# Caps, norms and residual adds of a fused attention block moved from VectorE to GpSimd

## The chip, the core and the metric

The kernel runs on one core of a Trainium2 chip. A core has TensorE (PE, the matrix engine, which writes to PSUM), VectorE (DVE) and GpSimd (POOL) for elementwise work, ScalarE (ACT) for activation functions, and SyncE (SP), whose queue issues most of the DMAs here. Each engine takes its own instructions in order; between engines they wait on semaphores. The metric is the device time of one execution in microseconds (us): the median of several runs.

## The reference

`x` is [1, 2048, 640] in bf16. Rows are normalised, and two branches work on the result: linear attention with 32 heads of 20 channels, and a dense network with a ReLU, 1728 wide, whose output goes through a SiLU and gates the attention.

```python
def _layernorm(x, axis=-1, eps=1e-5):
    m = jnp.mean(x, axis=axis, keepdims=True)
    v = jnp.var(x, axis=axis, keepdims=True)
    return (x - m) / jnp.sqrt(v + eps)
...
        phi = lambda t: jnp.where(t > 0, t + 1, jnp.exp(t)) + 1e-6
        pq, pk = phi(q), phi(k)
        kv = jnp.einsum("bhsd,bhse->bhde", pk, v)
        z = jnp.einsum("bhsd->bhd", pk)
        num = jnp.einsum("bhqd,bhde->bhqe", pq, kv)
        den = jnp.einsum("bhqd,bhd->bhq", pq, z)[..., None] + 1e-6
        o = num / den
...
    xn = _layernorm(x, axis=-1)
    s = _A_ref(xn, A_wqkv, A_wo)
    g = _silu(_B_ref(xn, B_w1, B_w2))
    return x + s * g
```

The kernel computes `phi(t)` as min(exp(t), 1) + 1e-6 + relu(t): ScalarE takes the exponential and the ReLU out of PSUM, one instruction makes the cap (the minimum and the small addend), and one adds the two parts.

## The kernel before

**Tiles.** The 2048 rows are 16 tiles `t` of 128 rows, and four chunks `j` of 512. Each tile of `x` is loaded, `bn_stats` (L469) and `bn_aggr` (L473) on VectorE give its mean and variance, GpSimd makes the reciprocal root with two small instructions (`rsv` L475, `rsy` L477), and `LN_norm` (L497) writes the normalised tile `xn`. A DMA from the SP queue (L546) transposes it to `xnT`. The first four tiles are centred early and transposed on TensorE instead.

**Keys.** `K_mm` (L556) multiplies a tile by the key weights into two PSUM banks. `K_exp` and `K_relu` (L569, ScalarE) write to one of three or four slots of `ek`, and `K_fin(t)` makes the cap in place (L585) and the sum into `pk` (L587). All of `pk` is read much later, by the sum over the keys (L756) and by the products of `xn` and `pk` (L882, from 105 us).

**Queries.** `Q_mm` (L609) does the same for a chunk and 128 channels: ScalarE writes the exponential to one of three slots `er` (L617) and the ReLU to `pqT` (L622), then `f_sum` makes the cap (L630) and the sum (L827, the line of the helper `tt` for every elementwise operation with two tensors).

**Strassen units.** The products are made with Strassen's method in a form of seven products: sums of input blocks (`h_S`, `h_T`, `g_S`, `u_S`, `o_S`, all recorded at L827) are formed on VectorE, and products are gathered in PSUM. The hidden layer has ten such units (`h_unit`, matmuls at L1036): four for the first half of the rows (33 to 60 us), six for the second (70 to 112 us). A unit has the steps `s1`, `s5`, `s6`, `s2`, `s7`, `s3`, `s4`. In `s6`, VectorE adds a saved product to a PSUM bank that the next products of `s7` and `s3` write again; in `s4` it makes another such sum and a ReLU. Between the steps the key products of a tile, a query product and pieces of other work are put in by hand, as lists: in the first four units `first` holds the norms of tiles 10 to 15 (with `post`), `misc` and `post` the statistics of tiles 11 to 15, and `rest` and `fill_` go on with this up to 96 us.

**The last stage.** From 128 us on, pairs of tiles go through the second layer (`U_steps`), ScalarE's SiLU gate (L1354) and the output product (`O_steps`), both in PSUM banks by the same seven steps (L882). `s_mult` (L1517) multiplies the output product in PSUM by the gate into one of three slots `tmpo`; `s_store` (L1522) adds the rows of `x`, which were loaded again to `xre`, into a slot `outb`, and a DMA from the SP queue stores them. The adds of a pair are put off to the first step of the next pair (`late`, `flush`). The last tile goes in three pieces, the first of which GpSimd adds and ScalarE's queue stores.

**Order and waits.** The class `Sched` records each operation on the engine named in the call, in the order of the calls, and derives the semaphore waits from the reads and writes that the call names. So the order on an engine is the order of the program, and moving an operation to another engine changes neither the order of the calls nor what each of them depends on.

Of the kernel before, what the change touches and what calls it, by code (L numbers as in the profile page):

```python
# [4 lines left out]
ALU = mybir.AluOpType  # L5
# [203 lines left out]
def bass_recurrent_scan__linear_attn_block__dense_activation_relu__prompt_kernel(  # L209
# [78 lines left out]
    def eks(t):  # L288
        return t % 4 if t < 8 else t % 3
# [63 lines left out]
    sc = Sched(nc, NDS)  # L353
    nds = [0]

    def dma(E, fn, R=(), W=(), extra=()):
        i = nds[0]
        nds[0] += 1
        return sc.dma(E, fn, i, R=R, W=W, extra=extra)

    def tok(t):
        return slice(P * t, P * (t + 1))

    def schunk(j):
        return slice(512 * j, 512 * (j + 1))
# [3 lines left out]
    def xs(t):  # L369
        return t if t < XR else (t - 4) % XR  # L370
# [114 lines left out]
    last_norm = [None]  # L485

    def LN_norm(t):
        if t >= 99:
            sc.op("POOL", lambda eng: eng.scalar_tensor_tensor(
                out=rsv[:, t:t + 1], in0=mv[:, t, 0:1], scalar=-1.0, in1=rsy[:, t:t + 1], op0=ALU.mult, op1=ALU.mult),  # L490
                R=[("mv", t), ("rsy", t)], W=[("rsv", t)])
            last_norm[0] = sc.op("ACT", lambda eng: eng.activation(
                out=xn[:, t, :], in_=xin[:, xs(t), :], func=ACTF.Identity, bias=rsv[:, t:t + 1],
                scale=rsy[:, t:t + 1]), R=[("xin", xs(t)), ("rsv", t), ("rsy", t)], W=[("xn", t)])
            xnT_dma(t)
            return
        last_norm[0] = sc.op("DVE", lambda eng: eng.tensor_scalar(  # L497
            out=xn[:, t, :], in0=xin[:, xs(t), :], scalar1=mv[:, t, 0:1], scalar2=rsy[:, t:t + 1],
            op0=ALU.subtract, op1=ALU.mult), R=[("xin", xs(t)), ("mv", t), ("rsy", t)], W=[("xn", t)])
        xnT_dma(t)  # L500
# [44 lines left out]
    def xnT_dma(t):  # L545
        dma("SP", lambda eng: eng.dma_start_transpose(  # L546
            xnT[:, t // 4, :, P * (t % 4):P * (t % 4 + 1)], xn[:, t, :]), R=[("xn", t)], W=[("xnT", t)])
# [33 lines left out]
    def K_fin(t):  # L581
        es = eks(t)
        e_ = ek[:, es, 0, :]
        r_ = ek[:, es, 1, :]
        sc.op("DVE", lambda eng: eng.tensor_scalar(out=e_, in0=e_, scalar1=1.0, scalar2=1e-6, op0=ALU.min, op1=ALU.add),  # L585
              R=[("ek_e", es)], W=[("ek_e", es)])
        sc.op("DVE", lambda eng: eng.tensor_tensor(out=pk[:, t, :], in0=e_, in1=r_, op=ALU.add),  # L587
              R=[("ek_e", es), ("ek_r", es)], W=[("pk", t)])
# [4 lines left out]
    def nextb():  # L593
        b = RB[ring[0] % len(RB)]
        ring[0] += 1
        return b
# [10 lines left out]
    def Q_mm(j, f, b=None):  # L607
        b = nextb() if b is None else b
        sc.group("PE", [(lambda eng, k=k: eng.matmul(ps[b], lhsT=wq[:, k, P * f:P * (f + 1)], rhs=xnT[:, j, k, :],  # L609
                                                     start=(k == 0), stop=(k == C - 1))) for k in range(C)],  # L610
                 R=[("wq",)] + [("xnT", 4 * j + q) for q in range(4)], W=[("ps", b)])
        es = qi[0] % NER
        qi[0] += 1
        e_ = er[:, es, :]

        def f_exp():
            sc.op("ACT", lambda eng: eng.activation(out=e_, in_=ps[b], func=ACTF.Exp), R=[("ps", b)], W=[("er_e", es)])  # L617

        plain = True

        def f_relu():
            sc.op("ACT", lambda eng: eng.activation(out=pqT[:, f, schunk(j)], in_=ps[b], func=ACTF.Relu), R=[("ps", b)],  # L622
                  W=[("pqT", j, f)], extra=hz(hSk[0:2]) if f == C - 1 and j > 1 else ())

        def f_both():
            f_exp()
            f_relu()

        def f_sum():
            sc.op("DVE", lambda eng: eng.tensor_scalar(out=e_, in0=e_, scalar1=1.0, scalar2=1e-6, op0=ALU.min,  # L630
                                                       op1=ALU.add), R=[("er_e", es)], W=[("er_e", es)])
            tt(pqT[:, f, schunk(j)], e_, pqT[:, f, schunk(j)], ALU.add, [("er_e", es), ("pqT", j, f)], [("pqT", j, f)])

        if plain:
            return f_both, f_sum

        def f_fin():
            sc.op("DVE", lambda eng: eng.tensor_scalar(out=e_, in0=e_, scalar1=1.0, scalar2=1e-6, op0=ALU.min,
                                                       op1=ALU.add), R=[("er_e", es)], W=[("er_e", es)])
            sc.op("DVE", lambda eng: eng.scalar_tensor_tensor(  # L640
                out=pqT[:, f, schunk(j)], in0=ps[b], scalar=1.0 + 1e-6, in1=e_, op0=ALU.add, op1=ALU.max),
                R=[("ps", b), ("er_e", es)], W=[("pqT", j, f)],
                extra=hz(hSk[0:2]) if f == C - 1 and j > 1 else ())

        return f_exp, f_fin
# [101 lines left out]
    def hz(keys):  # L747
        return sc._hazards([], keys)
# [77 lines left out]
    def tt(out, in0, in1, op, R, W, extra=()):  # L826
        sc.op("DVE", lambda eng: eng.tensor_tensor(out=out, in0=in0, in1=in1, op=op), R=R, W=W, extra=extra)  # L827
# [268 lines left out]
    def run(ops):  # L1096
        for op_ in ops:
            op_[0](*op_[1:])

    S, N, F, SH, ZS, T0 = LN_stats, LN_norm, K_fin, h_S, scale_h, h_T  # L1100
    after = [[(S, 5), (N, 4)], [(S, 6), (N, 5)], [(S, 7), (N, 6)], [(F, 0), (N, 7)], [(F, 1)]]
    for n, f in enumerate(HP):
# [44 lines left out]
    for i, u in enumerate(units):  # L1147
        ob = 4 * (i % 2)
        t = 8 + i
# [327 lines left out]
    def O_steps(p):  # L1477
        t0, t1 = pairs[p]
        key = lambda q: ("oS", p % 2, q)
        base = ubase(p)  # L1480

        def prod(i):
            q_ = lambda half, t: [pqT[:, 2 * half + k, tok(t)] for k in range(2)]
            w_ = lambda half, n: [wf[:, 2 * half + k, HN * n:HN * (n + 1)] for k in range(2)]
            s_ = lambda q: [o_Sv(p, q)[:, k, :] for k in range(2)]
            t_ = lambda q: [oT[q][:, k, :] for k in range(2)]
            last = lambda t, n: [(pqT[:, 4, tok(t)], wf[:, 4, HN * n:HN * (n + 1)])]
            z = lambda a, b: list(zip(a, b))
            return {
                1: lambda: (z(q_(0, t0), w_(0, 0)), qk(t0, 0, 2) + wkeys),  # L1490
                2: lambda: (z(q_(1, t0), w_(1, 0)) + last(t0, 0), qk(t0, 2, 5) + wkeys),
                3: lambda: (z(s_(4), w_(1, 1)) + last(t0, 1), [key(4)] + qk(t0, 4, 5) + wkeys),
                4: lambda: (z(q_(1, t1), t_(4)) + last(t1, 0), qk(t1, 2, 5) + wkeys + [("oT", 4)]),
                5: lambda: (z(s_(1), t_(1)), [key(1), ("oT", 1)]),
                6: lambda: (z(s_(2), t_(2)), [key(2), ("oT", 2)]),
                7: lambda: (z(s_(3), t_(3)), [("oS3", p), ("oT", 3)]),
                8: lambda: (last(t1, 1), qk(t1, 4, 5) + wkeys),
            }[i]()

        def out_(q, b, s5=None, skey=None):  # L1500
            if q == 12:
                s_out(t0, base + 2)
            elif q == 21:
                s_out(t1, base)
            elif q == 22:
                tt(ps[b][:, 0:HN], ps[b][:, 0:HN], s5, ALU.add, [("ps", b), skey], [("ps", b)])

        return seven(base, prod, out_, 2 + p % 2, lo8, prod(8))
# [9 lines left out]
            out=tmpo[:, os_, lo:hi].rearrange(shp, a=na), in0=src, in1=g_of(t)[0][:, lo:hi].rearrange(shp, a=na),  # L1518
            op=ALU.mult), R=keys + [("g", gslot[t], 0), ("g", gslot[t], 1)], W=[("tmpo", os_, i)])

    def s_store(t, os_, pieces, lo, hi, E="DVE", D_="SP"):
        sc.op(E, lambda eng: eng.tensor_tensor(out=outb[:, os_, lo:hi], in0=tmpo[:, os_, lo:hi],  # L1522
                                               in1=xre[:, t, lo:hi], op=ALU.add),
              R=[("tmpo", os_, i) for i in pieces] + [("xre", t // 4)], W=[("outb", os_, lo)])
        dma(D_, lambda eng: eng.dma_start(out2[tok(t), lo:hi], outb[:, os_, lo:hi]), R=[("outb", os_, lo)])
# [13 lines left out]
    def s_out(t, b):  # L1539
        os_ = so[0] % NOUT  # L1540
        so[0] += 1
        s_mult(t, os_, 0, 0, D, ps2(b, HN), [("ps", b), ("ps", b + 1)], 2)
        late.append(lambda: s_store(t, os_, (0, ), 0, D))
# [7 lines left out]
    def s_last(t):  # L1551
        for i in range(3):
            lo, hi = LC[i], LC[i + 1]
            s_mm(t, lo, hi, LB[i])
            s_mult(t, NOUT, i, lo, hi, ps[LB[i]][:, 0:hi - lo].unsqueeze(1), [("ps", LB[i])], 1)
            if i == 0:
                s_store(t, NOUT, (0, ), lo, hi, "POOL", "ACT")
        s_store(t, NOUT, (1, 2), LC[1], D)
# [45 lines left out]
    for p in range(8):  # L1604
        us = U_steps(p)
        os_ = O_steps(p - 1) if p else None
# [90 lines left out]
```

## Time and profile before

| what | us |
|---|---|
| median of 3 runs (208.2 to 208.42) | 208.39 |
| span of the profiled execution, from its first to its last instruction | 207.0 |
| TensorE busy | 203.6 |
| VectorE busy | 169.7 |
| ScalarE busy | 124.3 |
| GpSimd busy | 18.0 |

The profile doesn't give the profiled execution a time of its own beside the span; the span is 1.4 us shorter than the median of the runs. By stretches of the span, busy us of each engine:

```profile
core 0: us, PE busy (x) PEld busy (x) DVE busy (x) ACT busy (x) POOL busy (x), PEclk, DMA share, GB/s
24.00:35.50 11.50, 11.50 (x76) 5.37 (x74) 10.09 (x26) 9.01 (x17) 3.27 (x6) 1.00 1.02 253
35.50:41.90 6.40, 6.40 (x35) 3.31 (x34) 5.51 (x15) 5.42 (x11) 0.95 (x2) 1.00 0.41 53
41.90:48.30 6.40, 6.40 (x35) 3.31 (x34) 5.89 (x15) 5.42 (x11) 0.00 (x0) 1.00 0.13 26
48.30:54.70 6.40, 6.40 (x35) 3.31 (x34) 5.50 (x15) 5.42 (x11) 1.58 (x4) 1.00 0.14 28
54.70:60.70 6.00, 6.00 (x33) 3.08 (x32) 4.78 (x13) 4.49 (x9) 2.50 (x10) 1.00 0.27 55
60.70:72.70 12.00, 12.00 (x68) 6.49 (x67) 9.42 (x26) 11.84 (x23) 0.00 (x0) 1.00 0.36 96
72.70:105.00 32.30, 32.30 (x216) 14.78 (x215) 24.93 (x52) 23.35 (x45) 0.00 (x0) 1.00 0.16 49
105.00:146.00 41.00, 41.00 (x314) 28.95 (x312) 35.64 (x55) 17.51 (x37) 0.00 (x0) 1.00 0.67 207
146.00:204.50 58.50, 58.50 (x436) 42.21 (x434) 47.88 (x102) 24.02 (x63) 0.32 (x1) 1.00 0.21 72
```

A row names a stretch from A to B, its length, the busy time and the number of instructions of each engine in it (PEld is TensorE's loading of weights), the clock granted to TensorE, the mean share in which the DMA engines were busy, and what they moved. In the other views a line of a timeline is start, duration, engine, source line, operation, output and inputs with shapes, and in brackets the idle time of the engine before it with what ended it.

### The profile page before, as it was taken

To read this page: it belongs to the slowest core of one execution; us is meant where nothing else is said; L and a number is where in the kernel's file an instruction comes from. 1 tells how busy PE (TensorE), PEld (TensorE's weight loads), DVE (VectorE), ACT (ScalarE), POOL (GpSimd) and SP (SyncE) were. 2 spreads that over 40 slices of the span, in tenths; PEclk is the share of its full clock that TensorE was granted. 3 is DMA by queue.
4 is the path that set the end of the run, shared out by engine and by line. 5 is a ranking of instruction groups with operands and counts; after the bars stand their busy time and mean duration, and the time that the engine had idled before them with its cause. 6 is when DMAs were issued, how large, how long until landed. Compare 5 with 4: busy or idle time off the path is not lost.

```text
span 207.0 us, 3745 instructions
## 1 busy us (share of the span) xinstructions
PE 203.6 (98%) x1400; PEld 126.3 (61%) x1400; DVE 169.7 (82%) x373; ACT 124.3 (60%) x251; POOL 18.0 (9%) x53
## 2 busy tenths in 40 slices
PE   8999999999999999999999999999999999999995
PEld 7755645545555444444456777777777777777773
DVE  4888997988969787686889669898888989897465
ACT  5598869888889987686563435462525354352531
POOL 3174032101330000000000000000000000000001
PEclk9999999999999999999999999999999999999999
DMA  6965999211037000302225999237931011010103
GB/s 194 331 190 117 255 203 275 42 32 29 6 63 198 25 3 0 127 0 57 74 63 114 251 357 384 90 108 234 371 129 63 3 63 46 21 63 0 63 5 127
DMA packets 32999, 24.74 MB, mean 119 GB/s; under 512 B 12757, under 2 KB 32981, under 8 KB 32981
## 3 DMA queue, kind: packets, MB, share of 16 engines
q1 hardware_dynamic: 31749, 23.13, 39.2%
q10 hardware_dynamic: 1232, 1.37, 1.9%
q8 instruction: 11, 0.18, 0.4%
q14 instruction: 7, 0.06, 0.1%
HBM read 15.81 MB, written 5.24 MB: 102 GB/s over the span
## 4 chain that ended last, share of the span: by engine, by line
PE 97%; DMA 1%; DVE 1%; issue 0%
PE psT L882 40%; PE psT L1036 19%; PE psT L556 11%; PE psT L609 11%; PE psT L658 6%; PE psT L1529 3%; PE psT L1580 2%; DMA reg<-in_A_x_dram 1%; PE psT L676 1%; PE psT L1320 1%; PE psT L530 1%; PE psT L1294 1%; PE psT L756 1%; PE psT L786 1%; PE psT L432 0%; DVE stats L469 0%
## 5 line engine op out<-in xcount | busy, mean ns | idle before, releaser
L882 PE MATMUL psT<-reg,regH 128*128 128x320 bf16 (+1 forms) x224 | 34.3, 299 | 0.0
L882 PE MATMUL psT<-reg 128*128 128x320 bf16 (+1 forms) x164 | 27.7, 299 | 0.0
L882 PEld LDWEIGHTS psT<-reg,regH 128*128 128x128 bf16 (+1 forms) x224 | 21.9, 98 | 8.6
L1354 ACT ACTIVATE wv_sb<-psT 128x320 bf16<-128x320 f32 x28 | 11.3, 436 | 25.2 <-PE psT L882 15.4
L609 PE MATMUL psT<-reg 128*128 128x512 bf16 x100 | 24.4, 379 | 0.0
L1036 PE MATMUL psT<-reg 128*128 128x512 bf16 x80 | 23.2, 379 | 0.0
L827 DVE TENSOR_TENSOR psT<-psT,reg 128x320 f32<-128x320 f32 x30 | 14.3, 493 | 9.3 <-PE psT L882 9.2
L889 ACT ACTIVATE psT<-psT 128x320 f32<-128x320 f32 x32 | 13.6, 426 | 11.2 <-PE psT L882 10.7
L882 PEld LDWEIGHTS psT<-reg 128*128 128x128 f16 (+1 forms) x164 | 16.0, 98 | 6.9 <-DVE regH L827 0.2
L889 ACT ACTIVATE reg<-psT 128x320 f32<-128x320 f32 (+1 forms) x24 | 10.4, 435 | 15.6 <-PE psT L882 13.6
L556 PE MATMUL psT<-reg 128*128 128x320 bf16 x120 | 17.9, 299 | 0.0
L1042 ACT ACTIVATE psT<-psT 128x512 f32<-128x512 f32 x20 | 11.9, 595 | 8.2 <-PE psT L1036 8.2
L569 ACT ACTIVATE regE<-psT 128x640 bf16<-128x640 f32 x24 | 15.6, 706 | 1.9 <-PE psT L556 1.2
L609 PEld LDWEIGHTS psT<-reg 128*128 128x128 bf16 x100 | 9.6, 98 | 11.6 <-issue 0.7
L1048 ACT ACTIVATE regH<-psT 128x512 bf16<-128x512 f32 (+1 forms) x24 | 14.5, 604 | 2.1 <-PE psT L1036 1.8
L556 PEld LDWEIGHTS psT<-reg 128*128 128x128 bf16 x120 | 11.5, 98 | 6.5 <-ACT regE L569 0.5
L469 DVE BATCH_NORM_STATS2 stats<-reg 128x6 f32<-128x320 bf16 x32 | 14.1, 475 | 1.3 <-DMA reg<-in_A_x_dram 1.3
L827 DVE TENSOR_TENSOR reg<-reg 128x1024 f16<-128x1024 bf16 (+6 forms) x17 | 13.5, 805 | 1.7 <-DMA reg<-in_B_w_dram 1.2
L882 PE MATMUL psT<-reg,pqT 128*128 128x320 bf16 (+1 forms) x72 | 14.7, 299 | 0.0
L1517 DVE TENSOR_TENSOR reg<-psT,wv_sb 128x640 bf16<-128x640 f32 (+2 forms) x16 | 11.8, 739 | 3.0 <-PE psT L882 1.8
L1036 PEld LDWEIGHTS psT<-reg 128*128 128x128 bf16 x80 | 7.7, 98 | 9.4 <-issue 0.4
L1522 POOL TENSOR_TENSOR reg<-reg 128x224 bf16<-128x224 bf16 x1 | 0.6, 607 | 144.0 <-DVE reg L1517 144.0
(143 smaller groups left out, 369.0 us busy)
## 6 DMA issues: line engine op xcount, KB each, us to landing
reg<-in_B_w_dram SPq DMA_DIRECT2D x12, 320.0 KB, 5.5
scr<-rden SPq DMA_DIRECT2D x4, 640.0 KB, 8.3
reg<-in_A_x_dram SPq DMA_DIRECT2D x4, 640.0 KB, 6.6
out_dram<-reg SPq DMA_DIRECT2D x15, 160.0 KB, 1.9
regE<-scr SPq DMA_DIRECT2D x3, 640.0 KB, 7.5
reg<-in_A_x_dram SPq DMA_DIRECT2D x4, 320.0 KB, 4.4
reg<-in_A_wo_dram SPq DMA_DIRECT2D x6, 160.0 KB, 3.3
reg<-in_A_x_dram SPq DMA_DIRECT2D x5, 160.0 KB, 5.5
```

The lines of the kernel that those rows point to most:

```text
L469: sc.op("DVE", lambda eng: eng.bn_stats(stats[:, t, a, :], xv[:, HN * a:HN * (a + 1)]), R=[("xin", xs(t))], W=[("stats", t, a)])
L556: fns.append(lambda eng, a=a, k=k, lhs=lhs: eng.matmul(ps[b + a][:, 0:HN], lhsT=lhs, rhs=wk[:, k, HN * a:HN * (a + 1)], start=(k == 0), st ...
L569: sc.op("ACT", lambda eng: eng.activation(out=o_.rearrange("p (a n) -> p a n", a=2), in_=ps2(b, HN), func=func, scale=scale), R=[("ps", b) ...
L609: sc.group("PE", [(lambda eng, k=k: eng.matmul(ps[b], lhsT=wq[:, k, P * f:P * (f + 1)], rhs=xnT[:, j, k, :], start=(k == 0), stop=(k == C ...
L658: sc.group("PE", [(lambda eng, k=k: eng.matmul(ps[b], lhsT=w1_col(k, P * f, P), rhs=src[:, k, :], start=(k == 0), stop=(k == C - 1))) for ...
L827: sc.op("DVE", lambda eng: eng.tensor_tensor(out=out, in0=in0, in1=in1, op=op), R=R, W=W, extra=extra)
L882: sc.group("PE", [(lambda eng, k=k, lhs=lhs, rhs=rhs: eng.matmul(ps[b][:, 0:HN], lhsT=lhs, rhs=rhs, start=(start and k == 0), stop=(k == n ...
L889: sc.op("ACT", lambda eng: eng.activation(out=dst, in_=ps[b][:, 0:HN], func=ACTF.Copy), R=[("ps", b)], W=[dkey], extra=extra)
L1036: sc.group("PE", [(lambda eng, k=k, lhs=lhs, rhs=rhs: eng.matmul(ps[b], lhsT=lhs, rhs=rhs, start=(start and k == 0), stop=(k == n - 1), sk ...
L1042: sc.op("ACT", lambda eng: eng.activation(out=dst, in_=ps[b], func=ACTF.Copy), R=[("ps", b)], W=[dkey], extra=extra)
L1048: sc.op("ACT", lambda eng: eng.activation(out=dst, in_=ps[b], func=ACTF.Relu), R=[("ps", b)], W=[("hT", j, f)])
L1517: sc.op("DVE", lambda eng: eng.tensor_tensor(out=tmpo[:, os_, lo:hi].rearrange(shp, a=na), in0=src, in1=g_of(t)[0][:, lo:hi].rearrange(shp ...
```

## The change

Four places name another engine; no order and no data changes.

- The norms of tiles 8 to 15 go to GpSimd (8 instructions of 128x640).
- The key caps of tiles 4 to 15 go to GpSimd (12 of 128x640).
- All query caps go to GpSimd (20 of 128x512).
- The residual adds of tiles 0 to 13 go to GpSimd (14 of 128x640).

The sums behind the caps, the statistics, and every operation that reads or writes PSUM stay where they were.

```diff
-        last_norm[0] = sc.op("DVE", lambda eng: eng.tensor_scalar(
+        last_norm[0] = sc.op("DVE" if t < 8 else "POOL", lambda eng: eng.tensor_scalar(
             out=xn[:, t, :], in0=xin[:, xs(t), :], scalar1=mv[:, t, 0:1], scalar2=rsy[:, t:t + 1],
             op0=ALU.subtract, op1=ALU.mult), R=[("xin", xs(t)), ("mv", t), ("rsy", t)], W=[("xn", t)])
         xnT_dma(t)
...
-        sc.op("DVE", lambda eng: eng.tensor_scalar(out=e_, in0=e_, scalar1=1.0, scalar2=1e-6, op0=ALU.min, op1=ALU.add),
+        sc.op("DVE" if t < 4 else "POOL", lambda eng: eng.tensor_scalar(
+            out=e_, in0=e_, scalar1=1.0, scalar2=1e-6, op0=ALU.min, op1=ALU.add),
               R=[("ek_e", es)], W=[("ek_e", es)])
...
         def f_sum():
-            sc.op("DVE", lambda eng: eng.tensor_scalar(out=e_, in0=e_, scalar1=1.0, scalar2=1e-6, op0=ALU.min,
+            sc.op("POOL", lambda eng: eng.tensor_scalar(out=e_, in0=e_, scalar1=1.0, scalar2=1e-6, op0=ALU.min,
                                                        op1=ALU.add), R=[("er_e", es)], W=[("er_e", es)])
...
-    def s_store(t, os_, pieces, lo, hi, E="DVE", D_="SP"):
+    def s_store(t, os_, pieces, lo, hi, E=None, D_="SP"):
+        E = E or ("POOL" if t < 14 else "DVE")
         sc.op(E, lambda eng: eng.tensor_tensor(out=outb[:, os_, lo:hi], in0=tmpo[:, os_, lo:hi],
                                                in1=xre[:, t, lo:hi], op=ALU.add),
```

## The prediction

> **What bounds the kernel now.** I read the page first, for who is busy and what the chain that ended last is made of.
>
> ```profile
> PE 203.6 (98%) x1400; PEld 126.3 (61%) x1400; DVE 169.7 (82%) x373; ACT 124.3 (60%) x251; POOL 18.0 (9%) x53
> ...
> PE 97%; DMA 1%; DVE 1%; issue 0%
> ```
>
> TensorE is busy 203.6 of 207.0 us and makes up 97% of the chain. In the chain in order of time it works without a gap from 4.49 to 204.51; only 4.5 us before and 2.5 us behind are anything else, and none of the moved instructions lies in them. A 128x512 matmul group of five takes 1.08 us all along, at a granted clock of 1.00. So relief of VectorE can shorten nothing; the change can only leave TensorE alone or make it wait. The question is which slack stands between the moved work and TensorE.
>
> Next I read the groups by line and shape, VectorE's (first fence) and GpSimd's (second): count, busy us, mean ns.
>
> ```profile
> L497 DVE TENSOR_SCALAR reg<-reg,mv,rsy 128x640 bf16<-128x640 bf16 x16 | 6.8, 436 | 1.7 <-POOL rsy L477 1.6
> L1522 DVE TENSOR_TENSOR reg<-reg 128x640 bf16<-128x640 bf16 x15 | 6.7, 484 | 0.0
> L630 DVE TENSOR_SCALAR regE<-regE 128x512 bf16<-128x512 bf16 x20 | 5.8, 289 | 2.9 <-ACT regE L617 2.8
> L585 DVE TENSOR_SCALAR regE<-regE 128x640 bf16<-128x640 bf16 x16 | 5.1, 320 | 0.0
> ```
>
> ```profile
> L477 POOL TENSOR_TENSOR rsy<-rsv,mhalf 128x1 f32<-128x1 f32 x16 | 10.0, 624 | 1.3
> L475 POOL TENSOR_SCALAR rsv<-mv 128x1 f32<-128x1 f32 x16 | 4.4, 278 | 40.1 <-DVE mv L473 40.1
> L1522 POOL TENSOR_TENSOR reg<-reg 128x224 bf16<-128x224 bf16 x1 | 0.6, 607 | 144.0 <-DVE reg L1517 144.0
> L445 POOL TENSOR_SCALAR_AFFINE_SELECT mh<-mh 128x160 f32<-128x160 f32 x1 | 0.4, 377 | 0.1
> ...
> L426 POOL TENSOR_SCALAR_AFFINE_SELECT ident<-ident 128x128 bf16<-128x128 bf16 x1 | 0.3, 292 | 0.2 <-POOL ident L425 0.2
> ```
>
> Last I read the timelines around the places where TensorE reads what VectorE writes. In each unit of the Strassen stage the add of `s6` (L827) must end before TensorE's seventh product, because both use the same PSUM bank. Unit 2, VectorE and then TensorE (start us, us):
>
> ```profile
> 48.33 0.70 DVE L827 TENSOR_TENSOR psT<-psT,wv_sb 128x512 f32<-128x512 f32 x1
> 49.38 0.45 DVE L497 TENSOR_SCALAR reg<-reg,mv,rsy 128x640 bf16<-128x640 bf16 x1 [0.34 <-POOL rsy L477]
> 49.74 0.32 DVE L585 TENSOR_SCALAR regE<-regE 128x640 bf16<-128x640 bf16 x1
> 50.09 0.49 DVE L587 TENSOR_TENSOR reg<-regE 128x640 bf16<-128x640 bf16 x1
> ```
>
> ```profile
> 48.78 1.24 PE L609 MATMUL psT<-reg 128*128 128x512 bf16 x5
> 49.86 0.59 PE L1036 MATMUL psT<-regX,reg 128*128 128x512 f16 x2
> ```
>
> The add ends at 49.03, the product starts at 49.86: 0.83 us of slack. Units 0, 1 and 3 have the same (36.22 to 37.05, 42.63 to 43.45, 55.44 to 56.26).
>
> **The change part by part: what leaves VectorE.** 12 caps of keys x 0.320, 20 caps of queries x 0.289, 8 norms x 0.436, 14 adds x 0.484 = 3.8 + 5.8 + 3.5 + 6.8 = 19.9 us. TensorE does not wait for any of it now, so its worth is 0.
>
> **What GpSimd gets.** The trace has no GpSimd tensor_scalar of this width. Its 128x1 row, undisturbed, takes 0.22 us. The slope per element from the affine selects, whose 128x1 row (L441) takes 187 ns, is (292-187)/127 = 0.83 ns for bf16 and (377-187)/159 = 1.2 ns for f32; the add of 128x224 gives (607-220)/223 = 1.74 ns. A cap or norm of 640 is then 0.22 + 640 x slope: 0.75, 0.98 or 1.33 us; a cap of 512 0.64, 0.83 or 1.11. They have one tensor input and are nearest to the one-input bf16 row; I take 0.80 and 0.68. The residual adds are the row of 224 itself: 0.22 + 640 x 1.74 = 1.33 us, at most 640/224 x 0.607 = 1.73. Together 20 x 0.80 + 20 x 0.68 + 14 x 1.33 = 48 us on an engine that was 18.0 us busy: room overall, but in order behind its other work.
>
> **What is queued.** GpSimd takes its list in order: rsv and rsy of a tile (0.31 + 0.55, L475 and L477), its norm, the cap of another tile, a query cap. VectorE's very next instruction behind each cap is the sum that reads it (L587, L827), so VectorE now stops there until GpSimd is through, and behind it stand bn_stats, the `s4` add and the next `s6` add. The norms' transposes (SP) wait for GpSimd too, 2.7 us to landing. The wo loads behind tile 15's norm are needed only at 129 us; the output stores behind the adds are needed by nobody but the output slots.
>
> **A hold between the two engines.** The trace shows that VectorE's SBUF-only instructions hold up GpSimd. VectorE's timeline, then GpSimd's:
>
> ```profile
> 29.64 0.69 DVE L827 TENSOR_TENSOR regE<-reg 128x1024 f16<-128x1024 bf16 x1
> 30.25 0.69 DVE L827 TENSOR_TENSOR regX<-reg 128x1024 f16<-128x1024 bf16 x1
> ```
>
> ```profile
> 29.76 0.65 POOL L475 TENSOR_SCALAR rsv<-mv 128x1 f32<-128x1 f32 x1 [3.04 <-DVE mv L473]
> 30.50 0.86 POOL L477 TENSOR_TENSOR rsy<-rsv,mhalf 128x1 f32<-128x1 f32 x1
> ```
>
> The 0.22 us instruction ran until 30.41, just behind the end of VectorE's at 30.33; the 0.57 us one took 0.86, begun in the second's time. Whether a long GpSimd instruction holds VectorE likewise, no row shows; its price lies between 0 and GpSimd's whole duration per meeting. The Trainium skill's "SBUF — State Buffer", section "Who interferes with whom", speaks against the change: a VectorE instruction with two SBUF inputs, or in a two-port mode, and a GpSimd instruction exclude each other for whole instructions, whichever came first. By that rule the sum would be the upper walk below, without it the lower.
>
> **The sum, two walks along both queues** (durations as above, waits as in the code). *No hold at all.* Up to unit 2 VectorE is on time, as the moved work returns what the waits take. From 48.5 on: rsv/rsy of tile 12 until 49.5, norm 50.3, cap 51.1, sum of keys 51.15 (50.09 before), bn_stats and bn_aggr, `s4` add 52.6; rsv/rsy 13 until 53.6, query cap 54.3, sum 54.35 (53.32 before), bn_stats, `s6` add 55.8 to 56.45 against the product at 56.26: TensorE waits 0.2. Behind it GpSimd's backlog (two norms, four key caps, five query caps, the mv6 masks of 1.2) ends at 70.3, and VectorE reaches the `s6` add of the next unit at 72.7, when TensorE has just fed it. Sum +0.2.
>
> *Full hold, both ways.* Tiles 6 and 7: rsv8, cap 6, norm 8 and cap 7 come one behind the other until 30.0, the sum of tile 7 runs at 30.05 (27.68 before), and the `s6` add of unit 0 ends at 37.7 against 37.05: 0.7. In unit 0 two query caps, norm 10 and cap 8 alternate with VectorE's sums, the `s6` add of unit 1 ends at 45.2 against 44.15: 1.05. Unit 2 just holds; unit 3: 0.6. Then caps, masks and norm 15 meet four sums of keys, five of queries, three scalings and four h_T adds (0.41, 0.35, 0.36 and 0.61 each): 6.9 us of VectorE's on top of some 12 of GpSimd's where 13 us lie between 60 and 73. TensorE waits 0.4 for tile 15's transpose, 0.4 and 1.3 for hT1 and hT2, 0.65 for the next `s6` add. Sum 0.7 + 1.05 + 0.6 + 0.4 + 0.4 + 1.3 + 0.65 = +5.1.
>
> I take the hold for the part beyond the fixed 0.22 us alone, 0.58 of 0.80 = 0.73, as the row held was held to VectorE's end: 0.2 + 0.73 x 4.9 = +3.8.
>
> **Later stages: nothing.** From 73 to 96 the query caps delay a sum by some 0.15 us (cap 0.68 beside the 0.60 relu that the sum awaits anyway); VectorE's idle times of 0.25 to 1.56 before its `s6` adds cover it, and without them it would cost 0.15 in each of four units. The residual adds start as soon as L1517 is done. In 163.4 to 165.2 VectorE reads PSUM, so the first add of a pair meets nothing; the second ends at 166.1 to 166.5, where VectorE was through with its own adds at 165.9. Those 0.2 to 0.6 us go into the idle 0.57 before 168.80. The last adds, of tiles 14 and 15, stay. The span of 207.0 lies 1.4 under the median run of 208.39, and I leave those 1.4 as they are: 208.4 + 3.8 = 212.2.
>
> **The rivals.** *Slack takes everything* (not slower). It needs that GpSimd doesn't hold VectorE and that a cap costs no more than 0.80; it decides in units 2 and 3, and there the 0.83 us must outlast a lateness that I put at 0.9 to 1.0. For it: POOL is 9% busy and many exponentials wait long before VectorE comes to them. Against it: VectorE is 86 to 92% busy in units 0 to 2 (5.51 to 5.89 of 6.40 us), and the held rows. It gives 208.4 to 208.6. *GpSimd becomes the bound*: a wide tensor_scalar costs like the add's slope, 1.33 and 1.11. Then one pass from `s6` add to `s6` add in unit 2 is 0.9 + 1.33 + 1.33 + 0.4 + 1.2 + 0.9 + 1.1 + 0.35 + 1.1 = 8.6 us against TensorE's 6.4, lost in two units (4.4), and the backlog behind is longer by 7 x 0.53 + 6 x 0.43 = 6.3, of which some 3.5 find no cover: +8, 216.4, with holds up to 222. For it: the only wide two-operand GpSimd row is that slow; against: all one-input rows are faster. *The residual adds stall the last stage*: from 1.7 us each on (165.9 - 164.8 + 0.57) they push the next pair's `s6` adds; at 2.5 us each of 7 pairs loses up to 0.8, 214. Against it: the row of 224.
>
> **How the numbers follow.** Hold and chain, 0.60, 212.2, of itself 209.5 to 215.5; GpSimd as the bound 0.20, 216 to 222; slack takes all 0.13; the last stage 0.04; a gain 0.03, for which no step of the profile speaks. The range 208.8 to 219.0 leaves out nearly all of the slack case and the gain, and the upper third of GpSimd as the bound, some 0.2. A measurement tells 0.2% (0.42 us) from no change: faster 0.03, same 0.12, slower 0.85.
>
> **What would show it.** Right: TensorE with gaps between 35 and 76 us and none behind; VectorE idle before L587 and the sums of queries with GpSimd as releaser; SBUF-only rows of VectorE longer than before, or late, while GpSimd runs. Wrong: caps well under 0.7 us and no idle VectorE (slack), caps above 1.1 (bound), or gaps behind 146 us (the adds).

## The result

The changed kernel takes 259.82 us (median of 4 runs, 258.12 to 261.02) against 208.4 beside it on the same chip: 1.2455 times as long, with a 95% interval of 1.2404 to 1.2506. The forecast was 212.2. The page of the profile after, in the lines that answer to those shown of before:

```profile
PE 219.1 (84%) x1400; PEld 129.7 (50%) x1400; DVE 162.6 (63%) x319; ACT 125.6 (48%) x251; POOL 128.7 (50%) x107
...
PEclk9999986965995986869679999999999999999999
...
PE 56%; POOL 32%; DVE 7%; issue 2%; ACT 1%; DVEq 0%
```

GpSimd has gone from 18.0 to 128.7 us of work and from nothing to 32% of the chain. TensorE has the same 1400 matmuls, and stands still for 40.7 us of the span of 259.8 where it stood for 3.4 of 207.0. It is also busy for 15.5 us more with the same matmuls: in the slices around its gaps the clock granted to it falls, to digits between 5 and 8 in the row PEclk, which gives it in tenths of full speed. What GpSimd's instructions take, by line and shape (count, busy us, mean ns, and the idle time before them with its releaser):

```profile
L631 POOL TENSOR_SCALAR regE<-regE 128x512 bf16<-128x512 bf16 x20 | 41.0, 2051 | 13.6 <-ACT regE L618 12.5
L585 POOL TENSOR_SCALAR regE<-regE 128x640 bf16<-128x640 bf16 x12 | 29.3, 2445 | 2.5 <-ACT regE L569 1.6
L497 POOL TENSOR_SCALAR reg<-reg,mv,rsy 128x640 bf16<-128x640 bf16 x8 | 21.1, 2643 | 0.6
L1524 POOL TENSOR_TENSOR reg<-reg 128x640 bf16<-128x640 bf16 x14 | 19.4, 1395 | 86.5 <-DVE reg L1518 86.4
```

A cap of a key takes 2.36 us where nothing disturbs it and 2.45 in the mean, a cap of a query 1.92 and 2.05, a norm 2.5 to 2.8; the prediction had 0.80, 0.68 and 0.80. The add of two tensors is where it was put: 1.40 against 1.33.

Unit 2 shows how that reaches TensorE. VectorE's timeline first, then GpSimd's, then TensorE's, from the `s6` add of unit 2 to that of unit 3:

```profile
67.39 0.67 DVE L828 TENSOR_TENSOR psT<-psT,wv_sb 128x512 f32<-128x512 f32 x1
73.53 0.49 DVE L588 TENSOR_TENSOR reg<-regE 128x640 bf16<-128x640 bf16 x1 [5.47 <-POOL regE L585]
73.94 0.88 DVE L469 BATCH_NORM_STATS2 stats<-reg 128x6 f32<-128x320 bf16 x2
...
78.09 0.43 DVE L828 TENSOR_TENSOR pqT<-regE,pqT 128x512 bf16<-128x512 bf16 x1 [2.14 <-POOL regE L631]
78.43 0.88 DVE L469 BATCH_NORM_STATS2 stats<-reg 128x6 f32<-128x320 bf16 x2
79.34 0.21 DVE L473 BATCH_NORM_AGGREGATE mv<-stats 128x2 f32<-128x12 f32 x1
79.47 0.67 DVE L828 TENSOR_TENSOR psT<-psT,wv_sb 128x512 f32<-128x512 f32 x1
```

```profile
67.55 0.24 POOL L475 TENSOR_SCALAR rsv<-mv 128x1 f32<-128x1 f32 x1 [2.61 <-DVE mv L473]
67.87 0.57 POOL L477 TENSOR_TENSOR rsy<-rsv,mhalf 128x1 f32<-128x1 f32 x1
68.55 2.51 POOL L497 TENSOR_SCALAR reg<-reg,mv,rsy 128x640 bf16<-128x640 bf16 x1
71.14 2.36 POOL L585 TENSOR_SCALAR regE<-regE 128x640 bf16<-128x640 bf16 x1
75.15 0.24 POOL L475 TENSOR_SCALAR rsv<-mv 128x1 f32<-128x1 f32 x1 [1.65 <-DVE mv L473]
75.47 0.57 POOL L477 TENSOR_TENSOR rsy<-rsv,mhalf 128x1 f32<-128x1 f32 x1
76.12 1.93 POOL L631 TENSOR_SCALAR regE<-regE 128x512 bf16<-128x512 bf16 x1
```

```profile
73.45 1.24 PE L610 MATMUL psT<-reg 128*128 128x512 bf16 x5
80.20 1.03 PE L1037 MATMUL psT<-regX,reg 128*128 128x512 f16 x2 [5.50 <-DVE psT L828]
```

VectorE and GpSimd work in turns. The root can't start before the statistics, the norm not before the root, the cap stands behind the norm, VectorE's sum waits for the cap, the next statistics stand behind the sum, and the next root waits for them. One round from `s6` add to `s6` add is 12.1 us (67.39 to 79.47), where TensorE has work for 6.4. It waits 5.50 us, and its next two matmuls of 512 columns take 1.03 instead of 0.59 us.

Where the time is lost is seen from marks in the chain that ended last, first before, then after:

```profile
105.48 1.09 PE psT L882 x8
```

```profile
158.22 1.09 PE psT L883 x8
```

The first product of `xn` and `pk` (x8) starts at 158.22 instead of 105.48, 52.7 us late. From there on nothing is lost: to the end of the span it is 101.5 us before and 101.6 after.

The turns are not the whole of it. The product behind the `s6` add of unit 3 starts at 80.20 instead of 56.26, so up to there 23.9 us are lost. That of unit 4 starts at 118.29 instead of 74.21, so another 20.1 us are lost between these two, and there GpSimd's list is nearly full. The stretch from 97 to 127 us, with GpSimd (POOL) as the fifth of the busy times:

```profile
97.00:127.00 30.00, 18.14 (x67) 7.37 (x67) 13.46 (x24) 11.83 (x22) 29.05 (x13) 0.78 0.12 36
```

GpSimd is busy for 29.05 of 30.00 us here, and for 35.09 of the 38.10 between the two products. There its total work sets the time more than the turns do.

### The profile page after: what moved, and what is told of

It is laid out like the page before. It is cut to its first block, busy times and chain, and to the rows that moved or that the text cites. A ratio compares the mean times of both kernels' runs of the same rounds, so it can differ in the third digit from the quotient of the medians.

```text
span 259.8 us, 3753 instructions
## 1 busy us (share of the span) xinstructions
PE 219.1 (84%) x1400; PEld 129.7 (50%) x1400; DVE 162.6 (63%) x319; ACT 125.6 (48%) x251; POOL 128.7 (50%) x107
## 4 chain that ended last, share of the span: by engine, by line
PE 56%; POOL 32%; DVE 7%; issue 2%; ACT 1%; DVEq 0%
PE psT L883 32%; POOL regE L585 11%; POOL regE L631 11%; POOL reg L497 7%; PE psT L1037 7%; PE psT L556 4%; PE psT L659 3%; PE psT L610 3%; DVE stats L469 2%; PE psT L1531 2%; PE psT L1582 2%; PE psT L432 2%; POOL rsy L477 1%; DVE reg L588 1%; DVE pqT L828 1%
## 5 line engine op out<-in xcount | busy, mean ns | idle before, releaser
L1524 POOL TENSOR_TENSOR reg<-reg 128x640 bf16<-128x640 bf16 (+1 forms) x15 | 20.0, 1343 | 88.3 <-DVE reg L1518 88.2
L631 POOL TENSOR_SCALAR regE<-regE 128x512 bf16<-128x512 bf16 x20 | 41.0, 2051 | 13.6 <-ACT regE L618 12.5
L588 DVE TENSOR_TENSOR reg<-regE 128x640 bf16<-128x640 bf16 x16 | 7.9, 492 | 40.4 <-POOL regE L585 40.2
L610 PE MATMUL psT<-reg 128*128 128x512 bf16 x100 | 27.0, 410 | 4.8 <-DVE regH L1052 4.8
L585 POOL TENSOR_SCALAR regE<-regE 128x640 bf16<-128x640 bf16 x12 | 29.3, 2445 | 2.5 <-ACT regE L569 1.6
L828 DVE TENSOR_TENSOR pqT<-regE,pqT 128x512 bf16<-128x512 bf16 x20 | 8.5, 425 | 30.3 <-POOL regE L631 30.3
L556 PE MATMUL psT<-reg 128*128 128x320 bf16 x120 | 21.8, 341 | 6.1 <-DMA reg<-reg 5.3
L1037 PE MATMUL psT<-reg 128*128 128x512 bf16 x80 | 26.3, 423 | 0.0
L1355 ACT ACTIVATE wv_sb<-psT 128x320 bf16<-128x320 f32 x28 | 11.3, 436 | 25.1 <-PE psT L883 15.5
L497 POOL TENSOR_SCALAR reg<-reg,mv,rsy 128x640 bf16<-128x640 bf16 x8 | 21.1, 2643 | 0.6
L556 PEld LDWEIGHTS psT<-reg 128*128 128x128 bf16 x120 | 13.0, 110 | 15.5 <-issue 6.8
L610 PEld LDWEIGHTS psT<-reg 128*128 128x128 bf16 x100 | 10.1, 104 | 18.5 <-DVE regH L1052 5.8
L1037 PE MATMUL psT<-regX,reg 128*128 128x512 f16 x20 | 7.3, 454 | 14.1 <-DVE psT L828 14.1
```

The costliest lines, as they stand in the source:

```text
L497: last_norm[0] = sc.op("DVE" if t < 8 else "POOL", lambda eng: eng.tensor_scalar(out=xn[:, t, :], in0=xin[:, xs(t), :], scalar1=mv[:, t, 0 ...
L556: fns.append(lambda eng, a=a, k=k, lhs=lhs: eng.matmul(ps[b + a][:, 0:HN], lhsT=lhs, rhs=wk[:, k, HN * a:HN * (a + 1)], start=(k == 0), st ...
L585: sc.op("DVE" if t < 4 else "POOL", lambda eng: eng.tensor_scalar(out=e_, in0=e_, scalar1=1.0, scalar2=1e-6, op0=ALU.min, op1=ALU.add), R= ...
L631: sc.op("POOL", lambda eng: eng.tensor_scalar(out=e_, in0=e_, scalar1=1.0, scalar2=1e-6, op0=ALU.min, op1=ALU.add), R=[("er_e", es)], W=[( ...
L1037: sc.group("PE", [(lambda eng, k=k, lhs=lhs, rhs=rhs: eng.matmul(ps[b], lhsT=lhs, rhs=rhs, start=(start and k == 0), stop=(k == n - 1), sk ...
```

## The experiments

**One part alone.** Four kernels each move one of the four parts; the edits are the four of the change, one at a time.

The residual adds:

> Only the residual adds of tiles 0 to 13 on GpSimd. Theory (the price of GpSimd's tensor_scalar, 2.36 us for 128x640 and 1.92 for 128x512, makes the loss, in the stages up to 150 us): the adds cost nothing, 208.4 within 0.4, though VectorE's first SBUF-only instruction behind each add is held up by about 1 us, as in the changed kernel. Rival (any long GpSimd instruction costs time through the hold on VectorE): 210 or more, some 0.3 us for each of 7 pairs.

208.21 us, 0.9983 (0.9952 to 1.0013): no difference that can be told. The theory held for this part.

The query caps:

> Only the 20 query caps on GpSimd, each 1.92 us. Theory: each sum of a query then starts 1.4 us later than the end of the ReLU that it now waits for, less the 0.8 us of slack, in most of ten units: 212 to 218. Rival (the loss of 51 us is a backlog on GpSimd that needs all parts together): below 210, because 41 us of work spread over 110 us leave GpSimd mostly idle.

218.86 us, 1.0496 (1.0433 to 1.0559), a little over the theory's upper end. VectorE waits 22.1 us in all for these caps; the rival fell.

The key caps:

> Only the 12 key caps of tiles 4 to 15 on GpSimd, each 2.36 us. Theory: the sums of tiles 6 and 7 wait for caps that begin only behind the reciprocal root of tile 8, then each unit loses 1 to 3 us: 214 to 226. Rival (backlog of all parts together): below 211.

217.15 us, 1.0406 (1.0342 to 1.0471), inside the theory's range.

The norms:

> Only the norms of tiles 8 to 15 on GpSimd, each about 2.5 us. Theory: only the transposes wait for them, with 4 us and more of room until tile 13; tile 15's comes about 1.4 us late: 208.4 to 212. Rival (each moved instruction costs what it takes longer on GpSimd): 8 x 2.1 = 17 us, 225.

210.21 us, 1.0073 (1.0043 to 1.0103), inside it too; TensorE waits 1.4 us for two of the transposes. Eight instructions that are 2.2 us longer each cost 1.6 us together: what a GpSimd instruction costs depends on who waits for it.

The four losses, each against the 208.62 of that set, are -0.4, 10.2, 8.5 and 1.6: 20 us of the 51. The rest comes only when the parts meet.

**Two parts together.**

> Query caps and key caps on GpSimd, norms and residual adds on VectorE. Alone they cost 10.2 and 8.5 us, the norms 1.6 and the adds nothing, 20 in all of the 51. Theory (one queue: each moved instruction lengthens the round from one tile's statistics over GpSimd's list back to VectorE, and what is over the slack is lost in every round): together well over their sum of 19, 232 to 245. Rival (the losses simply add, and the rest of the 51 comes from the lower clock that long waits bring): 226 to 229.

242.81 us, 1.164 (1.1574 to 1.1707): 34 us where the parts alone make 19. The theory's range held it. Adding the norms, which cost 1.6 alone, and the residual adds, which cost nothing alone, costs another 17 from here to the changed kernel. So the parts add up in GpSimd's list, and VectorE waits behind the list.

**The price.** The caps with one operation in place of two (the key cap's line; the query cap's changes likewise):

```diff
-            out=e_, in0=e_, scalar1=1.0, scalar2=1e-6, op0=ALU.min, op1=ALU.add),
+            out=e_, in0=e_, scalar1=1.0, scalar2=None, op0=ALU.min),
```

> The changed kernel with caps on GpSimd that take the minimum alone; the addend 1e-6 of those caps is left out. Theory (GpSimd pays per element and operation): a cap of 640 falls from 2.36 us to 1.2 to 1.5 and one of 512 from 1.92 to 1.0 to 1.2, and the time from 260 to 218 to 235. Rival (the price is that of a tensor_scalar whatever it does): caps and time as in the changed kernel, 258 to 262.

The caps took 1.81 and 1.50 us undisturbed, so the second operation costs a little under a quarter of the price, and less came off than the theory had said: 241.02 us, over its 235. Its direction held: caps that are 0.55 and 0.42 us shorter make 12 x 0.55 + 20 x 0.42 = 15 us, GpSimd's busy time falls by 18.3 (from 128.7 to 110.4, as the disturbed caps shorten by more), and the time by 18.8.

The prices by themselves, on an unused buffer where GpSimd is otherwise idle and VectorE goes on with its work (`two_` is minimum and add, `one_` the minimum, `jf` the buffer read as f32, `h0` and `h1` its halves):

```diff
+    price(lambda eng: eng.tensor_scalar(out=junk, in0=junk, **two_))
+    price(lambda eng: eng.tensor_scalar(out=junk, in0=junk, **one_))
+    price(lambda eng: eng.tensor_scalar(out=jf, in0=jf, **two_))
...
+    price(lambda eng: eng.tensor_scalar(out=h1, in0=h0, **two_))
+    price(lambda eng: eng.tensor_scalar(out=h0, in0=h0, **two_))
+    price(lambda eng: eng.tensor_copy(h1, h0))
+    price(lambda eng: eng.tensor_tensor(out=h1, in0=h0, in1=h1, op=ALU.add))
```

> The kernel before with 24 GpSimd instructions on an unused buffer of 128x384, behind the mv6 masks, where GpSimd has nothing to do: three each of minimum and add in place on bf16 (384), minimum alone (384), the same two on f32 (192), minimum and add on bf16 from one half to the other and in place (192), a copy (192), an add of two tensors (192). Theory (GpSimd pays per element, and for every operation): with the rows of 512 and 640 so far, 2.36 - 1.92 over 128 columns is 3.4 ns per element for two operations and 1.81 - 1.50 is 2.4 for one, so 384 should take 1.5 and 1.1 us, 192 of two operations 0.8 and an add of two tensors 0.55; f32 costs per element as bf16 does. Rival (the price goes by bytes, or by working in place): f32 of 192 costs as much as bf16 of 384, or the instruction between the halves costs much less than the one in place.

GpSimd's groups in that kernel; L1183 is two operations, L1184 one, L1185 and L1186 the same on f32, L1187 between the halves, L1188 in place, L1179 the fill of the buffer:

```profile
L1183 POOL TENSOR_SCALAR wv_sb<-wv_sb 128x384 bf16<-128x384 bf16 x3 | 4.7, 1570 | 0.3
...
L1184 POOL TENSOR_SCALAR wv_sb<-wv_sb 128x384 bf16<-128x384 bf16 x3 | 3.6, 1188 | 0.2
L1185 POOL TENSOR_SCALAR wv_sb<-wv_sb 128x192 f32<-128x192 f32 x3 | 2.8, 925 | 0.2
L1187 POOL TENSOR_SCALAR wv_sb<-wv_sb 128x192 bf16<-128x192 bf16 x3 | 2.7, 903 | 0.2
L1186 POOL TENSOR_SCALAR wv_sb<-wv_sb 128x192 f32<-128x192 f32 x3 | 2.6, 859 | 0.2
L1188 POOL TENSOR_SCALAR wv_sb<-wv_sb 128x192 bf16<-128x192 bf16 x3 | 2.6, 852 | 0.2
L1189 POOL COPY wv_sb<-wv_sb 128x192 bf16<-128x192 bf16 x3 | 1.7, 570 | 0.2
L1190 POOL TENSOR_TENSOR wv_sb<-wv_sb 128x192 bf16<-128x192 bf16 x3 | 1.7, 569 | 0.2
...
L1179 POOL MEMSET wv_sb<- 128x384 bf16 x1 | 0.4, 418 | 0.0
```

The price goes by elements, some 3.1 to 3.7 ns each for two operations ((1570 - 852)/192 and (2.36 - 1.57)/256). The bytes and working in place matter little: f32 of 192 columns takes 0.93 us against 0.85 to 0.90 for bf16, far from the 1.57 of as many bytes. What the second operation adds is no fixed share: 0.38 us on 384 columns of bf16, 0.07 on 192 of f32. A one-input tensor_scalar is dearer per element than an add of two tensors (0.85 against 0.57 on 192 columns), and the fill of 384 columns costs about a quarter of it (0.42 against 1.57). The kernel took 209.03 us in a single run, against 208.13 beside it; one run can't tell whether the added work cost anything.

**Order in the list.** The norm behind the key cap instead of ahead of it:

```diff
-    after = [[(N, 8), (F, 7), (SH, 0, 4)], [(S, 9), (T0, 1, 0), (T0, 3, 0)], [(N, 9), (T0, 2, 0)],
+    after = [[(F, 7), (SH, 0, 4)], [(N, 8), (S, 9), (T0, 1, 0), (T0, 3, 0)], [(N, 9), (T0, 2, 0)],
...
+        K_fin(t)
         run(first[i])
-        K_fin(t)
```

> The changed kernel with the norms of tiles 8 and 10 to 14 recorded behind the key cap of the same step and not ahead of it; all instructions stay on their engines. Theory (what counts is what stands in GpSimd's list between a tile's statistics and the sum that VectorE waits in): each of five rounds loses up to 2.6 us of that list, of which the part that then delays the next root comes back: 248 to 256. Rival (GpSimd's total work sets the time, whatever the order): 258 to 262.

253.51 us, 1.2199 (1.2159 to 1.224), some 6 us under the changed kernel, with the same instructions on the same engines. VectorE's waits for key caps, first in the changed kernel, then here (us in total, times, longest):

```profile
DVE reg L588 <- POOL regE L585: 40.2, 11, 7.9
```

```profile
DVE reg L588 <- POOL regE L585: 24.8, 11, 2.9
```

So what stands ahead of a cap in the list counts, and the rival fell for the kernel as a whole. It holds in one stretch: most of the gain is there by the product of unit 3 (74.82 instead of 80.20), and from it to that of unit 4 both kernels need much the same, 36.9 and 38.1 us, with GpSimd busy for over 35 of them.

**TensorE's clock.** Matmuls that keep TensorE busy in two of its long waits. The expectation calls the bank that they write to idle, but `s4` gathers in it, so that part of the hidden layer is changed; the amount of other work is the same.

```diff
         e2, f2 = Q_mm(*qfill[i], ob)
+        if i in (1, 3):
+            bw = 4 * ((i + 1) % 2)
...
+            sc.group("PE", [(lambda eng: eng.matmul(ps[bw][:, 0:P], lhsT=one, rhs=one, start=True, stop=True))
+                            for _ in range(100 if i == 1 else 80)], W=[("ps", bw)])
         u["s7"]()
```

> The changed kernel with 100 and 80 matmuls of 128x128 into an idle PSUM bank (5.3 and 4.3 us at full clock) put where TensorE waits 6.7 and 5.5 us for the s6 add of units 1 and 3; nothing reads them. Theory (GpSimd's and VectorE's chain sets the time there, TensorE's clock hardly): the granted clock behind these two waits rises from 0.7 to 0.8 towards 1.0, and the time falls by 0 to 4 us, 256 to 260. Rival (the lower clock is a loss of its own, 15.5 us of TensorE's busy time in all): 252 or less.

Three stretches (start and end, length, then busy us of each engine, and behind POOL's count the granted clock), first of the changed kernel, then of this one:

```profile
48.50:58.50 10.00, 3.29 (x20) 1.59 (x19) 3.38 (x8) 2.82 (x6) 8.00 (x6) 0.77 0.08 16
58.50:68.30 9.80, 9.19 (x35) 3.77 (x36) 5.25 (x12) 5.74 (x10) 6.81 (x5) 0.71 0.08 17
...
80.30:97.00 16.70, 11.69 (x54) 5.74 (x53) 2.77 (x7) 9.48 (x17) 14.33 (x15) 0.81 0.12 25
```

```profile
48.50:58.50 10.00, 8.76 (x113) 7.18 (x114) 3.38 (x8) 1.90 (x4) 8.00 (x6) 1.00 0.09 18
58.50:68.30 9.80, 6.82 (x30) 3.22 (x29) 5.35 (x12) 5.14 (x10) 6.84 (x6) 0.83 0.08 17
...
80.30:97.00 16.70, 9.32 (x52) 4.83 (x51) 2.77 (x7) 9.59 (x17) 14.33 (x14) 1.00 0.15 29
```

The clock behind the waits came up from 0.71 to 0.83 and from 0.81 to 1.00, and the time stayed: 260.33 us against 259.82. In the last stretch GpSimd is busy 14.33 of 16.70 us in both kernels; TensorE, faster, waits longer. Behind these two waits the slow clock is a companion of the wait and not a loss of its own; in the others it was not raised by itself.

**Waits and holds apart.** The kernel before, with VectorE doing everything that it did, and GpSimd doing instructions of about the same length that nobody reads (98.9 us in all, for 91.4 us of caps and norms in the changed kernel):

```diff
+    def dummy(ns, extra):
+        for n in ns:
+            sc.op("POOL", lambda eng, n=n: eng.tensor_scalar(
+                out=junk[:, 0:n], in0=junk[:, 0:n], scalar1=1.0, scalar2=1e-6, op0=ALU.min, op1=ALU.add),
+                R=[("junk",)], W=[("junk",)], extra=extra)
...
+        if t >= 4:
+            dummy((384, 236), [sc.res[("ek_e", es)].w])
...
+            dummy((384, 110), [sc.res[("er_e", es)].w])
```

> The kernel before, in which VectorE makes all caps, norms and adds, and GpSimd does instructions of the same total length on an unused buffer at the same places of its list (each cap or norm of 640 as 384 and 236 columns, each cap of 512 as 384 and 110), which nothing reads. What is left of the change is GpSimd's occupancy: the roots of tiles 8 to 15 come late behind it, and VectorE is held up at the shared reads. Theory (the direct waits of the sums for their caps make most of the loss): 212 to 230. Rival (holds between the engines make it): 240 or more, as every hold is still there.

230.37 us, 1.1025 (1.0957 to 1.1094), just over the theory's upper end. Without any sum waiting for a cap of GpSimd's, 22 of the 51 us remain. VectorE's norms (L508) wait 22.6 us in all for the roots, which stand behind the idle work in GpSimd's list:

```profile
DVE reg L508 <- POOL rsy L486: 22.6, 8, 4.9
```

This doesn't yet tell late roots from holds, so the same again with nothing ahead of the last root:

> As e8_dummies, but the instructions on the unused buffer are left out up to the root of tile 15, so that no root stands behind one; from there on 18 pairs of them, some 40 us, run beside VectorE. What is left is the hold between the two engines alone. Theory (holds cost next to nothing, the waits and the late roots make the loss): 208 to 210. Rival (holds make a good part of the 22 us that e8_dummies lost): 212 or more.

208.67 us, 1.0031 (1.0006 to 1.0056). GpSimd is busy for 42.7 us with these instructions, almost without a break from 62 to 108 us, beside a VectorE that has its whole list, and they cost 0.6 us, at most 1.2. Holds are there, and VectorE's spare time takes them: the sum over the inputs of unit 4 (`h_T`), for instance, starts later than before, and the `s6` add behind it at 73.29 instead of 72.69, still before TensorE needs it. VectorE's busy time is 3.5 us longer than before here (173.2 against 169.7) and 7.0 longer in the kernel ahead of it (176.7), so holds on VectorE can be some 7 of the 22 us there at the very most, and the larger part are late roots. What this leaves open is the hold up to 62 us, where VectorE has least time to spare and where no run has it alone. Nor are the 22 us a share of the 51: in the changed kernel the norms that need those roots are GpSimd's own, VectorE waits 0.8 us for roots, and it waits 40.2 and 30.3 us for key and query caps.

## Why the prediction was wrong

**TensorE has nothing to gain, and the change can only make it wait: right.** TensorE was gapless before, and the span's 52.8 us more are 37.3 of standing still and 15.5 of matmuls at the lower clock.

**The price of a wide tensor_scalar: wrong, and the step that failed.** The prediction said of the caps and norms that "they have one tensor input and are nearest to the one-input bf16 row; I take 0.80 and 0.68". That row was an affine select of 128 columns, with 0.83 ns per element. Measured were 2.36 and 1.92 us, 3.4 ns per element ((2.36 - 1.92)/128). The norms took 2.64 us in the mean where 0.80 was put. The row was near in its operands only; caps with a single operation still took 1.81 and 1.50 us, 2.4 ns per element. The upper bound was wrong too. It was the add of two tensors, 1.33 us, on the view that one input can't cost more than two, and nothing in the trace had said that. A trace in which GpSimd does no wide tensor_scalar gives no upper bound for one.

The Trainium skill's "GPSIMD Engine Reference", section "4.1 Engine selection", puts one-input elementwise work on GpSimd at about line rate and two-input work at about half of VectorE's. These runs disagree: 192 columns of two operations took 0.85 us and the two-input add of as many 0.57, VectorE's own cap of 640 columns takes 0.320 against GpSimd's 2.36, and its add of 640 takes 0.484 against GpSimd's 1.40. The measurement decides.

**The chain behind the caps: right as a mechanism.** The prediction named the order in GpSimd's list, the sum that waits behind each cap and what stands behind it, and its rival "GpSimd becomes the bound" had the right rounds: one pass of 8.6 us against TensorE's 6.4 with caps of 1.33. With the measured prices (2.51 to 2.64 for the norm, 2.36 to 2.45 for the key cap, 1.92 to 2.05 for the query cap) the same sum gives 11.6 to 12.0, near the 12.1 that unit 2 shows. The rival also had the backlog behind the units. It put the loss at 4.4 us in two rounds and 3.5 of backlog; 23.9 us were lost up to unit 3's product and 20.1 more up to unit 4's. It got 0.20 and an upper end of 222, as it had the same price bound.

**The hold as the main term: wrong.** Of the 3.8 us forecast, 3.6 were the hold between the two engines (0.73 x 4.9). The kernel with 42.7 us of late, unread GpSimd work lost 0.6 us, with an interval that ends at 1.2. The hold exists, and behind 62 us VectorE's slack covers it. Up to there no run has it alone, but the traces bound it: taken one by one in their order, VectorE's 319 instructions of the changed kernel last 9.9 us longer than the same ones before, 4.6 of it up to 158 us and 5.3 behind, where nothing is lost. GpSimd's 40 caps and norms last some 4.7 us longer in their means than undisturbed. Beside 51 us lost, both are small.

**The later stages: half right.** The residual adds cost nothing, as forecast, in the changed kernel and alone, although VectorE's instructions beside them became 5.3 us longer in all. The query caps from 73 us on were put at 0.15 us behind the ReLU; by their length alone they end 1.3 us behind it (1.92 us against the 0.60 of the ReLU), and the last of them releases VectorE's sum only at 149.23. Tile 15's transpose, put at 0.4 us late, lets TensorE wait 5.3.

**Rivals.** "Slack takes everything" needed caps of 0.80 and fell with the price; that no gain was in sight held.

## What to carry to other kernels

Before elementwise work is moved to GpSimd, get the price of that very operation, at its width, from a trace; a fill, a select or a 128x1 row is no stand-in, and 3.4 ns per element is seven times what VectorE's cap takes here. Then write down the round: if what GpSimd gets stands between two things that the other engine does in order, its whole list counts once per round, and parts that are nearly free alone (1.6 us for the norms) can cost ten times that together. Then add up its list over each stretch too: where it is nearly full (29.05 of 30.00 us here), the list itself sets the time. What hangs on nobody's round, as the residual adds with three slots behind them, moves for nothing, and gains nothing either while another engine has no gap.

## What the runs showed beyond that

The hold differs with the operation. Two moments of VectorE's timeline after, the first beside a residual add of GpSimd's, the second beside a query cap, and then GpSimd's side of both:

```profile
200.04 1.39 DVE L828 TENSOR_TENSOR reg<-reg,pqT 128x256 f16<-128x256 f16 x1
```

```profile
106.59 1.10 DVE L828 TENSOR_TENSOR regE<-reg 128x1024 f16<-128x1024 bf16 x1
107.61 0.68 DVE L828 TENSOR_TENSOR regX<-reg 128x1024 f16<-128x1024 bf16 x1
```

```profile
106.22 2.23 POOL L631 TENSOR_SCALAR regE<-regE 128x512 bf16<-128x512 bf16 x1
...
199.89 1.40 POOL L1524 TENSOR_TENSOR reg<-reg 128x640 bf16<-128x640 bf16 x1 [0.36 <-DVE reg L1518]
```

VectorE's sum of 256 columns, 0.29 us elsewhere, lasts until 201.43, just behind the end of GpSimd's add at 201.29: held for the whole add. Beside the cap, the first sum takes 1.10 instead of 0.69 us, and the second runs its usual 0.68 and is over at 108.29, while the cap goes on to 108.45. The Trainium skill's "SBUF — State Buffer", section "Who interferes with whom", has the later of two such instructions blocked for the whole of the earlier one. The add agrees; the cap, of which only the first part holds VectorE up at this moment, does not. Why the two differ, no run shows.
